# Transposing x by DMA instead of on TensorE for the last five blocks, in a fused window attention and squared-ReLU FFN

## The chip, the cores and the metric

The kernel runs on one core of a Trainium2 chip. The metric is device time in microseconds (us): the median of three runs before the change is 312.11 us (311.29 to 312.19). One more execution was profiled. It took 310.89 us, of which 309.2 us are the span from its first to its last instruction.

## The reference

Causal attention with a window of 64 over 8 batches, 8 heads, 576 positions and a head size of 64 is followed by a feed-forward layer without biases whose activation is the square of a ReLU:

```python
# q, k, v: (8, 8, 576, 64)
scores = (1/8) * q @ k.T                      # masked to 0 <= i - j < 64
attn   = softmax(scores)
x      = (attn @ v).transpose(0, 2, 1, 3).reshape(4608, 512)
out    = maximum(x @ w_in, 0)**2 @ w_out      # w_in 512 x 2048, w_out 2048 x 512
```

The inputs and the output are float32; the kernel works in float16 with float32 sums.

## The kernel before, in words

The 4608 rows are cut into nine blocks of 512 rows, counted from 0 in the code and here. Blocks 0 to 7 are the first 512 positions of each batch; block 8 gathers the last 64 positions of all eight batches. A block's attention consists of four units (g, hp), one for each pair of heads.

A unit passes through these steps. `Sc` forms the scores on TensorE and their exponential on ScalarE. `M` applies the mask on VectorE. `AV` multiplies by v on TensorE. `N` divides by the sum of each row on VectorE and writes the tile `xs`, 128 x 512 in float16, of which there are three buffers. `X` then turns `xs` around: four 128 x 128 transposes on TensorE into PSUM (L323) and one copy of 128 x 512 to the SBUF tile `xT` on ScalarE (helper line L111). `xT[g][:, hp, :]` is the hp-th quarter of the contraction of the first FFN product.

The FFN of a block has 16 groups `F1(g, f)` and 16 groups `F2(g, ts, quarter)`. Each group is four matmuls of 512 columns. An F1 group (L337) needs all four quarters of `xT[g]` in the order of hp; VectorE then takes the ReLU (`hr`, L340) and ScalarE the square (`h2`, L341). Four F2 groups (L372) make one 128 x 512 tile of the output, which ScalarE copies to `osb` (L376, five buffers) and SyncE stores (L362).

The order of all engines is written out by hand. The main loop has passes n = 1 to 8, called stages here. Stage n fills 32 places, counted i = 0 to 31, with the 16 F2 groups of block n and the 16 F1 groups of block n+1, in an order such as `"2222" + "11" + 2 * "212121211" + "21221211"` (1 for F1, 2 for F2). So the first F1 group of a stage stands at place 4. Attention work of block n+2 is put ahead of certain places: `Sc` of units 0 and 1 at place 8, their `AV` and `N` at 14, their `X` at 18 and 20; `Sc` of units 2 and 3 at place 18, their `AV` and `N` at 24, their `X` at 28 and 30. The x of block n+2 is therefore finished in stage n, and stage n+1 reads it from place 4 on.

Three kinds of DMA share the one in-order queue of SyncE (called SP in the profile): loads of the parts of q, k and v (L198, L201, L205), DMA transposes of the cast q and k parts of blocks 3 to 8 (`transpose_part`, L231, 128 x 512 in float16 each), and stores of `osb` (L362). `next_part` issues a load, queues its cast on GpSimd (POOL in the profile), and issues the transpose of the part that was loaded four parts earlier; that transpose waits on SP for the cast. About 14.5 parts are issued in each stage until the 80th part in stage 5. GpSimd does the casts in order, and the shifted copies of v (six a block) between them.

Before the main loop, block 0's F1 groups run in a stage of their own, with the transposes of q and k of block 1's first two units (`T`, L243: eight transposes on TensorE and one copy of 128 x 1024 on ScalarE for unit 0, on VectorE for unit 1) ahead of groups 12 and 14. The change's title counts that block from one, as block 2, and counts block 4 as the fifth.

Of the kernel before, what the change touches and what calls it, by code (L numbers as in the profile page):

```python
# [9 lines left out]
FP16 = mybir.dt.float16  # L10
# [5 lines left out]
def kernel(  # L16
# [6 lines left out]
    moe_w_out: bass.AP,  # L23
    out: bass.AP,
):

    nc = tc.nc  # L30
# [3 lines left out]
    P = 128  # L34
    HP = H // 2
    NBLK = B + 1
    DMC = DM // P
# [12 lines left out]
    xtpool = ctx.enter_context(tc.tile_pool(name="xtpool", bufs=2))  # L50
# [4 lines left out]
    ps_f1 = ctx.enter_context(tc.tile_pool(name="ps_f1", bufs=2, space=bass.MemoryType.PSUM))  # L55
# [53 lines left out]
    def copy(engine, out, in_):  # L109
        if engine is nc.scalar:  # L110
            engine.activation(out=out, in_=in_, func=AF.Copy, scale=1.0)  # L111
        else:
            engine.tensor_copy(out=out, in_=in_)  # L113
# [120 lines left out]
    pm, av, xs, xT = {}, {}, {}, {}  # L234
    at_ps = [ps_at.tile([P, 2, 512], FP32, name=f"at{i}") for i in range(2)]

    def T(g, hp, pool=ps_tr, tag="tr", engine=nc.scalar):

        qkt = apool.tile([P, 2, 512], FP16, name="qk", tag="qk")
        tr = pool.tile([P, 2, 512], FP16, name="tr", tag=tag)  # L240
        for a, what in enumerate("qk"):
            for i in range(4):
                nc.tensor.transpose(out=tr[:, a, i * P:(i + 1) * P],  # L243
                                    in_=p16[what, g, hp][:, i * P:(i + 1) * P], identity=ident[:])
        copy(engine, qkt[:].rearrange("r a (p i) -> r a p i", i=4),
             tr[:].rearrange("r a (i p) -> r a p i", i=4))
        qT[g, hp, "unit"], kT[g, hp, "unit"] = qkt[:, 0, :], qkt[:, 1, :]
# [36 lines left out]
    def M(g, hp):  # L284
        p = pm[g, hp]
        m0 = 1 if g == B else 0
        m = mask[:, m0:m0 + 8, :].rearrange("p j r -> p (j r)")
        nc.vector.tensor_tensor(out=p[:], in0=p[:], in1=m.unsqueeze(1).broadcast_to([P, 2, 512]),  # L288
                                op=ALU.min)
# [27 lines left out]
    def X(g, hp, engine=nc.scalar, pool=ps_tr, tag="tr"):  # L317

        if g not in xT:
            xT[g] = xtpool.tile([P, DMC, 512], FP16, name="xT", tag="xT")  # L320
        tr = pool.tile([P, 2, 512], FP16, name="xtr", tag=tag)
        for jp in range(4):
            nc.tensor.transpose(out=tr[:, 0, jp * P:(jp + 1) * P], in_=xs[g, hp][:, jp, :, :],  # L323
                                identity=ident[:])
        copy(engine, xT[g][:, hp, :], tr[:, 0, :])


    h2 = {}

    def F1(g, f, pool=ps_f1, tag="f1", into=None):  # L330
        if g not in h2:
            h2[g] = h2pool.tile([P, FFC, 512], FP16, name="h2", tag="h2")
        hps, done = open_f1.pop((g, f), (None, 0))
        if hps is None:
            hps = into if into is not None else pool.tile([P, 512], FP32, name="hps", tag=tag)
        for c in range(done, DMC):
            nc.tensor.matmul(hps[:], w_in_sb[:, c, f * P:(f + 1) * P], xT[g][:, c, :],  # L337
                             start=(c == 0), stop=(c == DMC - 1))
        hr = opool.tile([P, 512], FP32, name="hr", tag="hr")
        nc.vector.tensor_scalar(out=hr[:], in0=hps[:], scalar1=0.0, scalar2=None, op0=ALU.max)  # L340
        nc.scalar.activation(out=h2[g][:, f, :], in_=hr[:], func=AF.Square)  # L341
# [26 lines left out]
    def F2(g, ts, quarter, pool, tag):  # L368
        if quarter == 0:
            f2[g, ts] = pool.tile([P, 512], FP32, name="ops", tag=tag)  # L370
        for f in range(4 * quarter, 4 * quarter + 4):
            nc.tensor.matmul(f2[g, ts][:], h2[g][:, f, ts * P:(ts + 1) * P], w_out_sb[:, f, :],  # L372
                             start=(f == 0), stop=(f == FFC - 1))
        if quarter == 3:
            osb = opool.tile([P, DM], FP32, name="osb", tag="osb", bufs=5)
            nc.scalar.activation(out=osb[:], in_=f2[g, ts][:], func=AF.Copy, scale=OUT_SCALE)  # L376
            to_store.append((g, ts, osb))
        if quarter == 1 or g == seq[-1]:
            while to_store:
                store(*to_store.pop(0))  # L380

    def F2_last(g, ts):

        for half, (pool, tag) in enumerate(((ps_f2, "f2"), (ps_f1, "f1"))):
            cols = slice(half * 256, half * 256 + 256)
            t = pool.tile([P, 512], FP32, name="ops", tag=tag)
            for f in range(FFC):
                nc.tensor.matmul(t[:, 0:256], h2[g][:, f, ts * P:(ts + 1) * P], w_out_sb[:, f, cols],  # L388
                                 start=(f == 0), stop=(f == FFC - 1))
            osb = opool.tile([P, DM], FP32, name="osb", tag="osb", bufs=5)  # L390
            nc.scalar.activation(out=osb[:, 0:256], in_=t[:, 0:256], func=AF.Copy, scale=OUT_SCALE)  # L391
            for par, queue in enumerate((nc.sync, nc.scalar)):
                r = (2 * ts + par) * S + 512
                queue.dma_start(out=out[r:r + 64, cols], in_=osb[par * 64:(par + 1) * 64, 0:256])

    seq = list(range(NBLK))
# [3 lines left out]
    with tc.manual_schedule():  # L400
        g0, g1, g2, g3 = seq[:4]
# [17 lines left out]
        dve, pool, act = nc.vector, nc.gpsimd, nc.scalar  # L419
# [59 lines left out]
        three = [in_f1, in_f1, in_f2]  # L479
# [6 lines left out]
            cast_qk_pair(g1, "q", hp, nc.gpsimd)  # L486
            cast_qk_pair(g1, "k", hp, nc.gpsimd)
        for f in range(FFC):
            if f == 12:
                T(g1, 0)  # L490
            if f == 14:
                T(g1, 1, engine=nc.vector)
            F1(g0, f, *three[f % 3])

# [50 lines left out]
        def A(g, hp, i=1):  # L547
            AV(g, hp, i)
            N(g, hp)
# [37 lines left out]
        for n in range(1, NBLK):  # L587
            g = seq[n]
            one = seq[n + 1] if n < NBLK - 1 else None
            if one is not None:  # L590
                first = [lambda f=f: F1(one, f) for f in range(FFC)]
                second = [lambda ts=ts, i=i: F2(g, ts, i, ps_f2, "f2") for ts in range(4) for i in range(4)]
                a, b = iter(first), iter(second)
                order = ("2222" + "11" + 2 * "212121211" + "21221211" if n > 1 else
                         "22222222" + 2 * "11211211212" + "11")
                fill = [next(a if c == "1" else b) for c in order]
            else:
                fill = [lambda ts=ts, i=i: F2(g, ts, i, *((ps_f2, "f2") if ts % 3 == 0 else (ps_f1, "f1")))
                        for ts in range(3) for i in range(4)] + [lambda: F2_last(g, 3)]
            at = {}  # L600

            def put(i, *work):
                at.setdefault(i, []).extend(work)

            if n == 1:
                put(0, lambda: Sc(g2, 3), lambda: A(g2, 2))
                put(2, lambda: M(g2, 3))
                put(3, lambda: X(g2, 2))
                put(4, lambda: A(g2, 3))
                put(6, lambda: X(g2, 3))  # L610
            for work in later:
                put(1, work)
            later = []
            base = 4 * (n + 2)
            for i, x, two in ((12 if n == 1 else 8, (9, 11) if n == 1 else (10, 12), units[base:base + 2]),
                              (21 if n == 1 else 18, (9, None) if n == 1 else (10, 12), units[base + 2:base + 4])):
                for t, u in enumerate(two):
                    if u is not None:
                        put(i, lambda u=u, t=t: Sc(*u, i=t))
                        put(i + 3 + t, lambda u=u: M(*u))  # L620
                        put(i + 6, lambda u=u, t=t: A(*u, i=t))
                        if x[t] is None:
                            later.append(lambda u=u: X(*u))
                        else:
                            put(i + x[t], lambda u=u: X(*u))
            for i, group in enumerate(fill):
                for work in at.pop(i, []):
                    work()
                total = 12 + (32 * (n - 1) + i + 1) * (len(load_list) - 12) // 150
                while done < total and (parts_left or pending):  # L630
                    next_part()
                    done += 1
                group()
            assert not at, at.keys()
# [30 lines left out]
```

## Time and profile before

| | |
|---|---|
| median of three runs | 312.11 us |
| profiled execution: time, span | 310.89 us, 309.2 us |
| TensorE (PE) busy | 299.9 us, 97% of the span |
| VectorE, ScalarE, GpSimd busy | 162.7, 171.6, 117.5 us |
| SP's DMA queue (q1): packets' time, share of 16 engines | 82.8% |
| granted TensorE clock, mean | 1.000 |

The stages 2 to 6 run from 106.9, 138.5, 169.8, 201.1 and 232.5 us of the span, one about 31.35 us after the other, and stage 7 from 263.8 us. TensorE is busy in all of each. The last load of a part is issued at 221.7 us, in stage 5; behind that SP has only stores.

### The profile page before, as it was taken

Reading aid. Unit: us, or ns where it says so; the run is one execution under the profiler, and the core shown is the slowest. Engines: PE = TensorE matmul, PEld = TensorE weight load, DVE = VectorE, ACT = ScalarE, POOL = GpSimd, SP = SyncE. Lnnn points to the kernel's source line nnn. Section 1 sums busy time; section 2 is a strip of 40 time slices with the busy share of each in tenths; the row PEclk is TensorE's granted clock in tenths of the full one; section 3 lists DMA queues with packets and bytes.
Section 4 is the critical chain, followed back from the end, with each engine's and each line's share of the span. In section 5 each row is a group of like instructions: output and inputs, shape, how many; then the busy total and the mean of one; then the engine's idle time right before and its main releaser. Section 6 shows DMA issues by size and latency. Waiting matters only on the chain.

```text
span 309.2 us, 6624 instructions
## 1 busy us (share of the span) xinstructions
PE 299.9 (97%) x2604; PEld 150.8 (49%) x2604; DVE 162.7 (53%) x278; ACT 171.6 (55%) x268; POOL 117.5 (38%) x212
## 2 busy tenths in 40 slices
PE   7899999999999999999999999999999999999995
PEld 5444445454445544544454444544554555444444
DVE  4676628587266727553755365537553655344300
ACT  4757736686367545753575367546744674444411
POOL 4578749963462382254365246322320000000000
PEclk9999999999999999999999999999999999999999
DMA  7999999999999998999998999999921001100023
GB/s 231 241 354 375 384 289 280 310 188 175 235 182 225 178 224 187 204 194 202 197 232 187 211 187 184 205 220 173 217 58 70 34 2 36 68 34 34 36 63 74
DMA packets 141759, 55.49 MB, mean 179 GB/s; under 512 B 125728, under 2 KB 134176, under 8 KB 141728
## 3 DMA queue, kind: packets, MB, share of 16 engines
q1 hardware_dynamic: 141568, 54.94, 82.8%
q8 instruction: 20, 0.33, 0.5%
q10 hardware_dynamic: 160, 0.13, 0.2%
q14 instruction: 11, 0.09, 0.1%
HBM read 38.80 MB, written 9.44 MB: 156 GB/s over the span
## 4 chain that ended last, share of the span: by engine, by line
PE 81%; ACT 0%; DVE 0%; issue 0%
PE hps L337 36%; PE ops L372 35%; PE at L304 3%; PE at L274 3%; PE xtr L323 2%; PE ops L388 1%; PE tr L243 0%; PE hps L353 0%; PE at L337 0%; ACT osb L376 0%; DVE xT L113 0%; ACT osb L391 0%
## 5 line engine op out<-in xcount | busy, mean ns | idle before, releaser
L340 DVE TENSOR_SCALAR hr<-hps 128x512 f32<-128x512 f32 x143 | 97.9, 689 | 107.6 <-PE hps L337 106.4
L341 ACT ACTIVATE h<-hr 128x512 f16<-128x512 f32 x144 | 90.3, 630 | 86.8 <-DVE hr L340 86.6
L337 PE MATMUL hps<-xT,w_in_sb 128*128 128x512 f16 x560 | 137.6, 379 | 0.2
L372 PE MATMUL ops<-w_out_sb,h 128*128 128x512 f16 x560 | 136.1, 379 | 0.3 <-ACT osb L376 0.3
L372 PEld LDWEIGHTS <-h 128*128 128x128 f16 x560 | 53.1, 98 | 61.5 <-issue 0.3
L337 PEld LDWEIGHTS <-w_in_sb 128*128 128x128 f16 x564 | 53.1, 98 | 59.2 <-issue 1.4
L113 POOL CAST v_ev<-st_v 128x512 f16<-128x512 f32 x34 | 23.5, 692 | 43.9 <-DMA st_v<-in_v_dram 43.9
L113 POOL CAST k<-st_k 128x512 f16<-128x512 f32 x36 | 23.1, 641 | 44.7 <-DMA st_k<-in_k_dram 44.4
L281 ACT ACTIVATE pm<-at 128x1024 f16<-128x1024 f32 x35 | 34.1, 1015 | 2.7 <-PE at L274 2.7
L376 ACT ACTIVATE osb<-ops 128x512 f32<-128x512 f32 x35 | 20.5, 587 | 25.2 <-PE ops L372 25.2
L314 DVE TENSOR_TENSOR xs<-at,rden 128x512 f16<-128x512 f32 x36 | 24.9, 691 | 1.2
L288 DVE TENSOR_TENSOR pm<-pm,mask 128x1024 f16<-128x1024 f16 x32 | 24.1, 768 | 2.5 <-ACT pm L281 2.5
L111 ACT ACTIVATE xT<-xtr 128x512 f16<-128x512 f16 x31 | 18.4, 593 | 8.1 <-PE xtr L323 8.1
L113 POOL CAST q<-st_q 128x512 f16<-128x512 f32 x31 | 18.3, 609 | 10.9 <-DMA st_q<-in_q_dram 8.8
L222 POOL CAST v_od<-st_v 64x512 f16<-64x512 f32 x30 | 19.0, 635 | 1.6
L304 PEld LDWEIGHTS <-pm 128*64 128x64 f16 x576 | 11.4, 110 | 8.8 <-issue 4.3
L323 PEld LDWEIGHTS <-xs 128*128 128x128 f16 x144 | 10.7, 98 | 7.5
L304 PE MATMUL at<-v_ev,pm 128*64 128x65 f16 x384 | 14.3, 198 | 0.0
L323 PE MATMUL xtr<-ident,xs 128*128 128x128 f16 x144 | 13.8, 219 | 0.0
L113 POOL CAST v_od<-st_v 64x384 f16<-64x384 f32 x23 | 12.3, 536 | 1.8 <-DMA st_v<-in_v_dram 0.7
L304 PE MATMUL at<-v_od,pm 128*64 128x65 f16 x192 | 10.4, 194 | 0.4 <-DVE v_od L113 0.3
L111 ACT ACTIVATE qk<-tr 128x1024 f16<-128x1024 f16 x7 | 7.1, 1013 | 5.5 <-PE tr L243 3.1
(55 smaller groups left out, 120.4 us busy)
## 6 DMA issues: line engine op xcount, KB each, us to landing
st_k<-in_k_dram SPq DMA_DIRECT2D x40, 256.0 KB, 3.9
st_q<-in_q_dram SPq DMA_DIRECT2D x32, 256.0 KB, 5.1
out_dram<-osb SPq DMA_DIRECT2D x32, 256.0 KB, 2.8
st_v<-in_v_dram SPq DMA_DIRECT2D x28, 256.0 KB, 3.8
st_w<-in_moe_w_out_dram SPq DMA_DIRECT2D x16, 256.0 KB, 5.4
st_v<-in_v_dram SPq DMA_DIRECT2D x24, 128.0 KB, 4.9
w_st<-in_moe_w_in_dram SPq DMA_DIRECT2D x4, 512.0 KB, 6.1
st_w<-in_moe_w_in_dram SPq DMA_DIRECT2D x8, 256.0 KB, 7.6
```

The source lines that it names most:

```text
L111: engine.activation(out=out, in_=in_, func=AF.Copy, scale=1.0)
L113: engine.tensor_copy(out=out, in_=in_)
L281: nc.scalar.activation(out=p[:, hh, :] if apart else p[:], in_=sc[hh] if apart else both[:], func=AF.Exp, scale=1.0 / float(D) ** 0.5)
L288: nc.vector.tensor_tensor(out=p[:], in0=p[:], in1=m.unsqueeze(1).broadcast_to([P, 2, 512]), op=ALU.min)
L304: nc.tensor.matmul(a[jj * 64:(jj + 1) * 64, hh, jp * VW:jp * VW + D + 1], pm[g, hp][:, hh, j * 64:(j + 1) * 64], vsel, start=True, stop=True)
L314: nc.vector.tensor_tensor(out=x[:].rearrange("p j h d -> p h j d"), in0=a[:, :, :, 0:D], in1=rden[:].unsqueeze(3).broadcast_to([P, 2, 4, D ...
L323: nc.tensor.transpose(out=tr[:, 0, jp * P:(jp + 1) * P], in_=xs[g, hp][:, jp, :, :], identity=ident[:])
L337: nc.tensor.matmul(hps[:], w_in_sb[:, c, f * P:(f + 1) * P], xT[g][:, c, :], start=(c == 0), stop=(c == DMC - 1))
L340: nc.vector.tensor_scalar(out=hr[:], in0=hps[:], scalar1=0.0, scalar2=None, op0=ALU.max)
L341: nc.scalar.activation(out=h2[g][:, f, :], in_=hr[:], func=AF.Square)
L372: nc.tensor.matmul(f2[g, ts][:], h2[g][:, f, ts * P:(ts + 1) * P], w_out_sb[:, f, :], start=(f == 0), stop=(f == FFC - 1))
L376: nc.scalar.activation(out=osb[:], in_=f2[g, ts][:], func=AF.Copy, scale=OUT_SCALE)
```

## The change

- In stages 2 to 6 (blocks 4 to 8, twenty units) `X` is replaced by `X_dma`: one DMA transpose on SP's queue, from `xs` straight into `xT`. It stands at places 16 and 17 for units 0 and 1 and at places 26 and 27 for units 2 and 3, ahead of the parts and stores of its place. The four TensorE transposes and the ScalarE copy of these units are gone.
- In block 0's F1 stage, `T` of block 1's units 0 and 1 is issued from inside `F1`, after the matmuls of groups 12 and 14 and before their ReLU and square, where it stood ahead of those matmuls.

```diff
+    def X_dma(g, hp):
+        if g not in xT:
+            xT[g] = xtpool.tile([P, DMC, 512], FP16, name="xT", tag="xT")
+        nc.sync.dma_start_transpose(
+            out=xT[g][:, hp, :].rearrange("p (j r) -> p j r", j=4),
+            in_=xs[g, hp][:].rearrange("p j h d -> p (j h d)"))
...
-    def F1(g, f, pool=ps_f1, tag="f1", into=None):
+    def F1(g, f, pool=ps_f1, tag="f1", into=None, then=None):
...
         for c in range(done, DMC):
             nc.tensor.matmul(hps[:], w_in_sb[:, c, f * P:(f + 1) * P], xT[g][:, c, :],
                              start=(c == 0), stop=(c == DMC - 1))
+        if then is not None:
+            then()
         hr = opool.tile([P, 512], FP32, name="hr", tag="hr")
...
         for f in range(FFC):
-            if f == 12:
-                T(g1, 0)
-            if f == 14:
-                T(g1, 1, engine=nc.vector)
-            F1(g0, f, *three[f % 3])
+            F1(g0, f, *three[f % 3], then={12: lambda: T(g1, 0), 14: lambda: T(g1, 1)}.get(f))
...
-                        if x[t] is None:
+                        if u[0] >= seq[4]:
+                            put(i + 8 + t, lambda u=u: X_dma(*u))
+                        elif x[t] is None:
                             later.append(lambda u=u: X(*u))
```

Before, `T` of unit 1 was copied by VectorE; in the new call it takes the default engine, ScalarE.

## The prediction

> **What bounds the kernel now.** I read the page first, for the busy shares and the chain that ended last, then the main stages window by window, then TensorE's timeline around the removed work, and last SP's own timeline and waits, because the change puts its work there.
>
> ```profile
> PE 299.9 (97%) x2604; PEld 150.8 (49%) x2604; DVE 162.7 (53%) x278; ACT 171.6 (55%) x268; POOL 117.5 (38%) x212
> DMA  7999999999999998999998999999921001100023
> PE hps L337 36%; PE ops L372 35%; PE at L304 3%; PE at L274 3%; PE xtr L323 2%; PE ops L388 1%; PE tr L243 0%; PE hps L353 0%; PE at L337 0%; ACT osb L376 0%; DVE xT L113 0%; ACT osb L391 0%
> L111 ACT ACTIVATE xT<-xtr 128x512 f16<-128x512 f16 x31 | 18.4, 593 | 8.1 <-PE xtr L323 8.1
> ...
> qT<-q SPq DMA_TRANSPOSE x24, 3.5
> ```
>
> TensorE is the bound: 97% busy, and the chain that ended last is matmuls throughout, the x transposes (L323) 2% of it. What leaves TensorE is time gained, as long as nothing makes it wait. But the row of DMA digits is full up to slice 29, and only then falls. The windows of stages 4, 5 and 6 say the same:
>
> ```profile
> 169.96:201.30 31.34, 31.34 (x273) 15.37 (x272) 16.49 (x28) 17.67 (x29) 13.26 (x23) 1.00 1.10 197
> 201.30:232.65 31.35, 31.35 (x273) 15.41 (x272) 17.14 (x28) 17.64 (x29) 8.39 (x14) 1.00 0.94 162
> 232.65:264.00 31.35, 31.35 (x273) 15.41 (x272) 16.50 (x28) 17.67 (x29) 0.00 (x0) 1.00 0.10 35
> ```
>
> The last columns are granted clock, DMA share and GB/s: the DMA engines have packets in flight all the time up to stage 5, almost none in stage 6. TensorE's timeline shows a removed step, and the one stall that the second part touches:
>
> ```profile
> 126.69 0.39 PE L323 MATMUL xtr<-ident,xs 128*128 128x128 f16 x4
> 126.91 1.03 PE L337 MATMUL hps<-xT,w_in_sb 128*128 128x512 f16 x4
> ```
>
> ```profile
> 28.97 0.40 PE L243 MATMUL tr<-ident,q 128*128 128x128 f16 x4
> 29.71 0.40 PE L243 MATMUL tr<-ident,k 128*128 128x128 f16 x4 [0.35 <-POOL k L113]
> ```
>
> Four transposes take 0.22 us from start to the next start. SP's timeline in stages 2 and 4 shows no slack of that kind:
>
> ```profile
> 136.18 1.68 SPq L198 DMA_DIRECT2D st_k<-in_k_dram  x1
> 139.93 1.19 SPq L231 DMA_TRANSPOSE qT<-q  x1
> ...
> 189.21 2.88 SPq L231 DMA_TRANSPOSE qT<-q  x1
> 192.14 0.57 SPq L205 DMA_DIRECT2D st_k<-in_k_dram  x1
> 192.81 1.21 SPq L231 DMA_TRANSPOSE qT<-q  x1
> 194.06 0.58 SPq L205 DMA_DIRECT2D st_k<-in_k_dram  x1
> 194.75 1.21 SPq L231 DMA_TRANSPOSE qT<-q  x1
> 196.05 0.52 SPq L362 DMA_DIRECT2D out_dram<-osb  x1
> 196.63 0.42 SPq L205 DMA_DIRECT2D st_k<-in_k_dram  x1
> ```
>
> SP issues without a pause. A load and a transpose take 1.92 us (192.14 to 194.06), the load with its gap 0.62, so a transpose costs SP 1.30 us. Three things stretch this: a wait for a cast on GpSimd (137.9 to 139.9), and issues held to several times their length (1.68, 2.88) while earlier transfers are still in flight. And SP is late: the store at 196.05 stands behind place 26 of stage 4, which TensorE began at 195.51, though its tile had been ready at 192.58. A queue with slack would have sent it then, as it does from stage 6 on.
>
> **The second part of the change.** Moving `T` behind group 12's matmuls takes away the 0.35 us that TensorE waits for GpSimd's cast of k; with the gaps about 0.4 us. For unit 1 the copy moves from VectorE (1.21 us at 32.55) to ScalarE (about 1.0, 30.22); its transposes start 0.2 us later than now, the copy ends at about 33.6, and the scores of unit 1 would be due at about 33.5. So they wait 0.1 to 0.3 us, and the squares of groups 14 and 15 come 1 us later, which is hidden: the first F2 groups read groups 0 to 3. Ends: 0.6 gained, or 0.2 lost if the scores wait longest. I take 0.4 gained.
>
> **The removed work.** 20 units x 0.22 us = 4.4 us off TensorE, all on the chain. Twenty ScalarE copies of 0.593 us go too; ScalarE is 55% busy and nothing waits for it there, so they count nothing. Together 4.8 us.
>
> **The added work.** Twenty transposes of 128 x 512, the shape of the q and k parts, so 1.30 us of SP each. The four of stage 6 are free: SP then waits for most of the stage. The other sixteen lie in a full queue. None waits long for `N`: SP is behind TensorE at places 16 and 17 and, once delayed, at 26 and 27 too. What is behind them is every later load, transpose and store. Loads come 14 places or more before their unit needs them, stores have five buffers; the first to be late is the x itself. Unit 3 of a block is issued at place 27 and read by the fourth matmul of place 4 of the next stage.
>
> The tightest place is the start of stage 5. In the row of 196.05 SP has reached place 26 of stage 4; the next issue is at 196.63. By then it will have issued 4 + 4 + 4 new transposes, 12 x 1.30 = 15.6 us: unit 3's issue ends at 212.2, and the shortest landing in this stretch is 1.2 us after the end of an issue, so 213.4. TensorE wants it at 204.59 (start of place 4) + 3 x 0.216 = 205.2, less 12 x 0.22 and 0.4 gained by then: 202.2. That is 11.2 us late if SP's stretched spots stay as they are.
>
> They can shrink. Between 122 (the first new issue) and 196 SP waits for casts 2.0 us (137.9) and 1.65 (162.5), and is held 1.7 (132.5), 1.35 (to 137.9), 0.55 (148), 2.4 (158 to 162), 1.3 (177) and 1.65 (189.2) beyond the plain length: 12.6 us in all. An added issue that falls into such a spot costs nothing. So the wait of TensorE lies between 0 (11.2 absorbed) and 11.2 us (none), and the change breaks even where 6.4 of the 12.6 us, half, are absorbed. I take three tenths, 3.8 us. The holds come from the DMA engines being full, and a transpose brings 0.55 us of its own there (in a string of landings a transpose comes 0.5 to 0.6 us behind the load before it), so at most 0.75 of 1.30 can vanish in a hold, and only about half of the new issues stand in or just ahead of one. The waits for casts move along, because the loads that feed those casts are delayed in the same queue. That gives 11.2 - 3.8 = 7.4 us.
>
> The same sum for stage 4 (store at 165.48, next issue 166.06, 8 new transposes, wanted at 171.7) gives 177.7, 6.0 late, less 2.9 = 3.1 us; this wait is part of the 7.4, since TensorE's waiting does not slow SP. For stage 3 it gives 0, for stage 6 at most 0.2 more.
>
> **Sum.** -4.8 + 7.4 = +2.6 us. The profiled execution would go from 310.89 to 313.5. The median is 1.2 us above that execution, so 312.1 becomes 314.7 us.
>
> On SP's price the Trainium skill, page "DMA: Bandwidth & Descriptors", section "Issuing engines are not separate DMA queues", says that the time a sequencer takes to start a DMA is usually small beside the DMA. The rows differ (1.21 us of issue, 0.55 us between landings). By that rule the twelve transposes would cost 12 x 0.55 = 6.6 us in place of 15.6, 2.2 late unabsorbed, and the time would be that of the first rival.
>
> **Rivals.**
> *SP takes it up (faster).* If over half of the 12.6 us is absorbed, TensorE waits under 4.8 us; with all of it, not at all, and the time is 312.1 - 4.8 = 307.3. For it: the new issues at places 26 and 27 of stage 2 stand right in the string of held loads and ahead of the wait of 139.93. Against it: SP was late at every store of stages 2 to 5 but two.
> *The waits also cost the clock.* No wait of TensorE after its first 1.5 us is longer than 0.5 us now. The forecast's two (3.1 and then 4.3) would be the first long ones. At its start TensorE issued 24 matmuls of 128 x 128 in 2.74 us, 0.114 each against 0.055 in the x transposes, and was slow for about 4 us. If it starts so again twice, 2 us are lost each time: 314.7 + 4 = 318.7. The Trainium skill, page "TensorE: Matmul & The Clock Gate", part 1, states that an idle window of about 3.4 us halves the clock; no run here shows it in mid-kernel.
> *The three `xs` buffers bind.* Unit 3's `N` reuses unit 0's buffer, so VectorE would wait for unit 0's transpose. In stage 4 by the same sums it lands at about 196.0, with `N` due at 195.5; F1's two PSUM banks cover that. It adds 1 to 2 us where SP absorbs nothing, 312.1 - 4.8 + 11.2 + 1.5 = 320.
>
> **How the numbers follow.** Forecast case (TensorE waits 6 to 11.2 us): 0.50, time 314.7, own range 313.2 to 318.5. SP takes it up: 0.29, 307.3 to 311.1. Near balance, within 0.3% (about 0.9 us, what a measurement of this kernel can tell from no change): 0.08. Clock or buffers on top: 0.13, 318.7 to 320. So faster 0.29, same 0.08, slower 0.63. The range 307.5 to 319 leaves out the last tail and a sliver at the low end.
>
> **What would show it.** Right: L323 falls from 144 to 64 matmuls; waits of TensorE at L337 for the DMA that writes `xT`, at the starts of stages 4 and 5, some 3 and 4 us; the last load issued well after 221.7 us; stage 6 about 0.9 us shorter. Wrong: no such waits and stages of 30.5 us (first rival); matmuls of an F1 group at 0.43 us behind a wait (second); VectorE's `xs` waiting for a DMA (third). If a new transpose costs SP much more or less than 1.30 us, the whole sum moves by twelve times that.

## The result, and the profile after

| | before | changed |
|---|---|---|
| median (lowest to highest), us | 312.15 (311.23 to 312.52), 6 runs | 316.01 (313.5 to 317.55), 6 runs |
| profiled execution: time, span, us | 310.89, 309.2 | 316.02, 314.1 |
| granted TensorE clock, mean, profiled execution | 1.000 | 0.989 |

The ratio of the times is 1.0126, with an interval of 1.008 to 1.0173: the changed kernel is 1.3% slower. The two profiled executions differ by 5.1 us, the medians by 3.9, because the profiled execution of before lay 1.2 us under its median and that of after lies on it.

The page of the changed kernel: busy time by engine, the slices of TensorE, its granted clock and the DMA engines, the last chain by line, and two groups.

```profile
PE 299.2 (95%) x2524; PEld 146.7 (47%) x2524; DVE 161.9 (52%) x277; ACT 162.9 (52%) x249; POOL 117.0 (37%) x212
PE   6999998999999999999999699969999999999995
PEclk9999999999999999999999799989999999999999
DMA  6999999999999999999999999999999022101123
PE hps L346 32%; PE ops L383 29%; DMA xT<-xs 3%; DMA st_q<-in_q_dram 3%; PE at L275 3%; PE at L305 3%; PE ops L399 1%; DVE hr L351 1%; PE xtr L324 1%; SPq L332 1%; DVE pm L289 1%; SPq L373 1%; SPq L232 1%; ACT h L352 1%; PE tr L244 0%
L346 PE MATMUL hps<-xT,w_in_sb 128*128 128x512 f16 x560 | 140.2, 383 | 5.9 <-DMA xT<-xs 5.5
L112 ACT ACTIVATE xT<-xtr 128x512 f16<-128x512 f16 x11 | 6.5, 594 | 5.6 <-PE xtr L324 5.6
```

TensorE issues 80 instructions fewer and is busy for about the same time, 299.2 against 299.9 us, although the removed transposes were worth 4.4. So some of the rest ran slower. The row of TensorE has two dips (slices 22 and 26, counted from 0; the starts of stages 4 and 5), the row of its granted clock has two in the same slices, the DMA row stays full for two slices longer, and ScalarE's copies into `xT` (L112) fall from 31 to 11. The last chain is no longer matmuls throughout: the new transpose (`DMA xT<-xs`) and SP's issues are in it.

Stages 4, 5 and 6 of the changed kernel, window by window (length, the busy time of each engine with its instructions, and at the end granted clock, DMA share, GB/s):

```profile
168.40:203.42 35.02, 32.38 (x257) 14.87 (x256) 17.53 (x28) 15.66 (x25) 13.84 (x24) 0.95 1.05 191
203.42:238.55 35.13, 32.33 (x258) 14.74 (x256) 16.63 (x28) 15.65 (x25) 8.96 (x16) 0.95 1.18 193
238.55:269.00 30.45, 30.45 (x257) 14.41 (x256) 16.50 (x28) 15.66 (x25) 1.23 (x2) 1.00 0.28 73
```

Each lasted 31.35 us before. Stage 6 is 0.90 us shorter: four units without their TensorE transposes, 4 x 0.22. Stages 4 and 5 are 3.7 and 3.8 us longer. TensorE's timeline at their starts (start, duration, operation; in brackets the idle time ahead of it and what ended that):

```profile
171.69 0.81 PE L346 MATMUL hps<-xT,w_in_sb 128*128 128x512 f16 x3
175.14 1.96 PE L346 MATMUL hps<-xT,w_in_sb 128*128 128x512 f16 x5 [2.64 <-DMA xT<-xs]
176.89 1.91 PE L383 MATMUL ops<-w_out_sb,h 128*128 128x512 f16 x4
...
206.71 0.59 PE L346 MATMUL hps<-xT,w_in_sb 128*128 128x512 f16 x2
208.07 0.38 PE L346 MATMUL hps<-xT,w_in_sb 128*128 128x512 f16 x1 [0.76 <-DMA xT<-xs]
210.26 2.29 PE L346 MATMUL hps<-xT,w_in_sb 128*128 128x512 f16 x5 [1.82 <-DMA xT<-xs]
```

In stage 4 three matmuls of the first F1 group run, and the fourth waits for unit 3's quarter of `xT`. In stage 5 the third waits too. The matmuls behind the waits are slow: four of L383 take 1.91 us, which take 1.03 elsewhere. The granted clock in windows around them says why:

```profile
175.50:178.90 3.40, 3.40 (x10) 1.18 (x8) 1.38 (x2) 1.26 (x2) 0.70 (x2) 0.50 0.88 174
179.00:182.40 3.40, 3.40 (x46) 1.69 (x45) 0.79 (x2) 1.78 (x3) 1.21 (x4) 1.00 1.11 264
209.60:213.00 3.40, 2.74 (x7) 1.01 (x7) 1.03 (x2) 0.63 (x1) 0.61 (x1) 0.51 0.78 172
213.10:216.50 3.40, 3.40 (x46) 1.71 (x45) 0.94 (x2) 1.70 (x3) 0.86 (x2) 1.00 1.27 224
```

Half clock for about 3.4 us, twice, and full clock behind it. On SP, around place 26 of stage 4 (its store is the one at 206.88, which before stood at 196.05):

```profile
203.94 1.20 SPq L232 DMA_TRANSPOSE qT<-q  x1
205.24 1.21 SPq L332 DMA_TRANSPOSE xT<-xs  x1
206.88 0.36 SPq L373 DMA_DIRECT2D out_dram<-osb  x1
207.35 1.29 SPq L332 DMA_TRANSPOSE xT<-xs  x1
208.68 0.57 SPq L206 DMA_DIRECT2D st_k<-in_k_dram  x1
```

The two new transposes (L332) cost SP 1.21 and 1.29 us, as much as one of q (1.20). The second is unit 3's of block 6. It lands at 210.22, and TensorE had begun place 4 at 206.71; it waits for unit 2's first, the transpose issued at 205.24, and then for this one.

**Where the time went.** I compared the start of every FFN group in the two profiled executions. TensorE is 0.15 us ahead at the start of stage 1, 0.22 by its end, and gains another 0.22 at each of the twenty places where a unit's transposes are gone (4.4 in all). It loses 0.45 us at place 4 of stage 3, 2.8 in the wait of stage 4, 1.7 at half clock behind it, 2.9 in the waits of stage 5, 1.4 at half clock, 0.4 at places 29 and 30 of stage 5, and 0.1 elsewhere: 9.7 lost, 4.7 gained, 5.0 in the sum. The spans differ by 4.9.

### The profile page after: what moved, and what is told of

It reads as the page before. It is cut to its first block, busy times and chain, and to the rows that moved or that the text cites. A ratio compares the mean times of both kernels' runs of the same rounds, so it can differ in the third digit from the quotient of the medians.

```text
span 314.1 us, 6501 instructions
## 1 busy us (share of the span) xinstructions
PE 299.2 (95%) x2524; PEld 146.7 (47%) x2524; DVE 161.9 (52%) x277; ACT 162.9 (52%) x249; POOL 117.0 (37%) x212
## 3 DMA queue, kind: packets, MB, share of 16 engines
q1 hardware_dynamic: 152448, 57.56, 86.9%
## 4 chain that ended last, share of the span: by engine, by line
PE 69%; DMA 6%; SPq 3%; DVE 2%; issue 1%; ACT 1%; POOL 0%; DVEq 0%; POOLq 0%
PE hps L346 32%; PE ops L383 29%; DMA xT<-xs 3%; DMA st_q<-in_q_dram 3%; PE at L275 3%; PE at L305 3%; PE ops L399 1%; DVE hr L351 1%; PE xtr L324 1%; SPq L332 1%; DVE pm L289 1%; SPq L373 1%; SPq L232 1%; ACT h L352 1%; PE tr L244 0%
## 5 line engine op out<-in xcount | busy, mean ns | idle before, releaser
L346 PE MATMUL hps<-xT,w_in_sb 128*128 128x512 f16 x560 | 140.2, 383 | 5.9 <-DMA xT<-xs 5.5
L383 PE MATMUL ops<-w_out_sb,h 128*128 128x512 f16 x560 | 137.3, 382 | 0.3 <-ACT osb L387 0.3
L346 PEld LDWEIGHTS <-w_in_sb 128*128 128x128 f16 x564 | 54.1, 98 | 70.4 <-issue 10.6
L383 PEld LDWEIGHTS <-h 128*128 128x128 f16 x560 | 53.4, 98 | 62.8 <-issue 2.4
L114 POOL CAST v_ev<-st_v 128x512 f16<-128x512 f32 x34 | 21.7, 638 | 49.6 <-DMA st_v<-in_v_dram 49.6
L282 ACT ACTIVATE pm<-at 128x1024 f16<-128x1024 f32 x35 | 34.1, 1013 | 2.8 <-PE at L275 2.8
L387 ACT ACTIVATE osb<-ops 128x512 f32<-128x512 f32 x35 | 20.6, 588 | 25.0 <-PE ops L383 25.0
L114 POOL CAST q<-st_q 128x512 f16<-128x512 f32 x31 | 19.1, 626 | 18.8 <-DMA st_q<-in_q_dram 15.7
L112 ACT ACTIVATE qk<-tr 128x1024 f16<-128x1024 f16 x8 | 8.1, 1016 | 5.4 <-PE tr L244 3.3
L112 ACT ACTIVATE xT<-xtr 128x512 f16<-128x512 f16 x11 | 6.5, 594 | 5.6 <-PE xtr L324 5.6
L312 DVE RECIPROCAL rden<-at 128x8 f32<-128x8 f32 x36 | 7.2, 200 | 3.7 <-PE at L305 3.5
L114 POOL CAST w_out_sb<-st_w 128x512 f16<-128x512 f32 x12 | 7.7, 642 | 3.1 <-DMA st_w<-in_moe_w_out_dram 2.7
```

Source lines behind the costliest of these rows:

```text
L282: nc.scalar.activation(out=p[:, hh, :] if apart else p[:], in_=sc[hh] if apart else both[:], func=AF.Exp, scale=1.0 / float(D) ** 0.5)
```

## The experiments

The theory after the result: SP's queue was full, each new transpose costs it a fixed time of issue, so the x of blocks 5 and 6 lands too late, and TensorE waits and then runs at half clock. Its rivals: that the transposes are late because of their bytes on the DMA engines and not because of their issue, that the clock would have fallen anyway, and that the moved `T` is what costs time. The kernel before ran beside every kernel, with medians of 312.15 (experiments 1 to 4), 311.98 (5 to 8) and 312.43 us (9 and 10).

**1. The moved `T` alone.** All x stays on TensorE.

```diff
-                        if u[0] >= seq[4]:
+                        if False:
```

> The changed kernel with x of all units transposed on TensorE as before, so that only the moved transposes of block 1 are left of the change. Theory: TensorE loses its 0.35 us wait at L243 and nothing else changes; in the trace of the changed kernel stage 1 begins 0.15 us earlier than before, so 311.7 to 312.1 us, no measurable difference. Rival: the two ScalarE copies ahead of the squares hold back later work, and this part of the change is to blame for some of the loss: 312.6 us or more.

Measured: 312.94 us (312.14 to 314.27), ratio 1.003 (1.0014 to 1.0046). It is not faster, against the forecast, and it lies outside the 311.7 to 312.1 us expected, in the range given for the rival (312.6 or more). TensorE's timeline of this kernel around the moved transposes:

```profile
30.33 0.39 PE L244 MATMUL tr<-ident,q 128*128 128x128 f16 x4
30.90 0.40 PE L244 MATMUL tr<-ident,k 128*128 128x128 f16 x4 [0.18 <-POOL k L114]
31.13 1.89 PE L346 MATMUL hps<-xT,w_in_sb 128*128 128x512 f16 x8
```

`T` stands 1.4 us later than before (28.97) and TensorE still reaches k before its cast is done, because in this execution GpSimd did that cast 1.2 us later (30.23 in place of 29.04). Stage 1 starts 0.5 us later than before, and the remaining 1.4 us of this execution's loss lie behind the last matmuls, where the last but one store took 2.58 us to issue on ScalarE's queue (0.56 before), which has nothing to do with `T`. In ten profiled executions of this study (all but experiment 9's) stage 1 starts anywhere from 0.15 us earlier to 1.5 us later than before, under both orders. A gain of 0.4 us can't be seen in that, and the rival isn't shown by it either.

**2. Each new transpose in two halves.** The same bytes, twice the issues.

```diff
-        nc.sync.dma_start_transpose(
-            out=xT[g][:, hp, :].rearrange("p (j r) -> p j r", j=4),
-            in_=xs[g, hp][:].rearrange("p j h d -> p (j h d)"))
+        for a in (0, 2):
+            nc.sync.dma_start_transpose(
+                out=xT[g][:, hp, a * P:(a + 2) * P].rearrange("p (j r) -> p j r", j=2),
+                in_=xs[g, hp][:, a:a + 2].rearrange("p j h d -> p (j h d)"))
```

> The changed kernel with each new DMA transpose issued as two of 128 x 256: the same bytes and packets, twice the issues on SP. Theory (SP's issue time is what runs out): each half still costs SP about 1.2 us, so unit 3 of block 6 lands about 12 x 1.2 = 14 us later than in the changed kernel, less what falls into holds; 324 to 332 us, with the waits at the starts of stages 4 to 6 several us longer. Rival (the DMA engines' time runs out): the bytes are the same, 315 to 318 us.

Measured: 336.6 us (335.24 to 337.6), ratio 1.0782 (1.0752 to 1.0812). SP's timeline of this kernel at place 26 of stage 4, then the wait of TensorE for `xT` (total, times, longest):

```profile
214.90 1.20 SPq L232 DMA_TRANSPOSE qT<-q  x1
216.15 0.58 SPq L206 DMA_DIRECT2D st_k<-in_k_dram  x1
216.82 1.21 SPq L232 DMA_TRANSPOSE qT<-q  x1
218.13 2.48 SPq L333 DMA_TRANSPOSE xT<-xs  x2
220.71 0.53 SPq L374 DMA_DIRECT2D out_dram<-osb  x1
```

```profile
PE hps L347 <- DMA xT<-xs: 19.4, 8, 4.7
```

Two halves take 2.48 us, 1.24 each, where a whole one takes 1.22. Sixteen extra issues in stages 2 to 5 are 20 us of SP, and TensorE's waits for `xT` grow from 5.5 to 19.4; more of it runs at half clock too (mean 0.959). The time is above the 324 to 332 us expected, which had counted twelve of the issues and no further loss of clock. No byte was added, and the packets of SP's queue took no longer on the DMA engines: 78.1% of 335.6 us is 262 us, against 86.9% of 314.1, or 273 us, in the changed kernel. So the issue on SP is what is scarce. The Trainium skill, page "DMA: Bandwidth & Descriptors", section "Issuing engines are not separate DMA queues", calls the time to start a DMA usually small beside the DMA itself; for this transpose the measurement decides otherwise.

**3. The stores of blocks 1 to 5 on ScalarE's queue**, to free SP of 20 stores.

```diff
-            nc.sync.dma_start(out=out[g * S + ts * P:g * S + (ts + 1) * P, :], in_=osb[:])
+            (nc.scalar if 1 <= g <= 5 else nc.sync).dma_start(
+                out=out[g * S + ts * P:g * S + (ts + 1) * P, :], in_=osb[:])
```

> The changed kernel with the stores of blocks 1 to 5 issued from ScalarE's queue in place of SP's. They use the same 16 DMA engines. Theory (SP's issue time): ten stores of 0.58 us stand ahead of the late transpose at the start of stage 5, so it comes 5.8 us earlier; of the 8.0 us by which it landed too late about 2 are left, too short to lose the clock: 308.5 to 311 us, clock 1.00. Rival (DMA engines): the same packets pass through the same engines, 315 to 317.5 us, waits as in the changed kernel.

Measured: 317.27 us (316.0 to 317.62), ratio 1.0158 (1.0137 to 1.0179). The expectation failed. ScalarE's timeline of this kernel in stage 1:

```profile
78.89 0.60 ACT L388 ACTIVATE osb<-ops 128x512 f32<-128x512 f32 x1 [0.27 <-PE ops L384]
86.69 0.39 ACTq L373 DMA_DIRECT2D out_dram<-osb  x1
87.12 0.60 ACT L112 ACTIVATE xT<-xtr 128x512 f16<-128x512 f16 x1 [7.64 <-DMA st_q<-in_q_dram]
```

The first store on ScalarE's queue was held until 86.6 us, when a load that SP had issued landed, and everything behind it on ScalarE stood for 7.64 us. In the trace that load and the store report their landing on the same semaphore, and the wait ahead of the store is for that semaphore: the program as built asked for it, and it is no property of ScalarE's queue. TensorE lost 3.9 us waiting for the `xT` copy and about 1.7 more at half clock. So from stage 2 on the kernel runs some 6 us later than SP's loads were planned for, and the disappearance of the wait in stage 4 can't be credited to the freed queue. As a test of SP this run is inconclusive.

**4. TensorE kept busy where it waits.** 13 and 20 matmuls without use ahead of place 4 of stages 4 and 5; they are extra work, their result goes nowhere.

```diff
+    def fill_pe(n):
+        t = ps_tr.tile([P, 512], FP32, name="fill", tag="tr")
+        for _ in range(n):
+            nc.tensor.matmul(t[:], ident[:], w_in_sb[:, 0, 0:512], start=True, stop=True)
...
+                if i == 4 and n in (4, 5):
+                    fill_pe({4: 13, 5: 20}[n])
```

> The changed kernel with idle TensorE time filled: 13 matmuls of 512 columns into a spare PSUM bank ahead of place 4 of stage 4 and 20 ahead of place 4 of stage 5, results unused. Theory (the slow matmuls behind each wait are the clock, lost by standing idle): the clock stays at 1.00 and the matmuls behind the waits keep 0.216 us. The first loss (1.7 us) is hidden in the lateness of the next transpose anyway, so about 1.4 us are won: 314.6 us against 316.0. Rival (matmuls behind a wait are slow for another reason, such as the transfers): they stay slow, and the fill adds up to 1 us: 316 to 317 us.

Measured: 314.46 us (313.89 to 315.55), ratio 1.0069 (1.005 to 1.0088), with a granted clock of 1.000 in every run. TensorE's timeline of this kernel at the start of stage 4:

```profile
172.91 2.97 PE L357 MATMUL fill<-w_in_sb,ident 128*128 128x512 f16 x13
175.71 2.02 PE L346 MATMUL hps<-xT,w_in_sb 128*128 128x512 f16 x8
177.57 1.03 PE L388 MATMUL ops<-w_out_sb,h 128*128 128x512 f16 x4
```

Behind the filler the four L388 matmuls take 1.03 us in place of 1.91. So the half clock follows from the waits and is not there anyway. By the medians, work without use makes the kernel 1.5 us faster than the changed one (316.01), though the intervals of the two ratios overlap a little. That is about the price of one of the two slow spells, not of both (3.1); the section on the prediction says why. In this execution, the slowest of the four at 315.55, the second filler ran too long: unit 3's x had landed at 210.24, and the fourth matmul of place 4 came at 211.26, so about 1.0 us of the gain was given away.

**5. The x transposes alone**, `T` put back where it was.

```diff
-            F1(g0, f, *three[f % 3], then={12: lambda: T(g1, 0), 14: lambda: T(g1, 1)}.get(f))
+            if f == 12:
+                T(g1, 0)
+            if f == 14:
+                T(g1, 1, engine=nc.vector)
+            F1(g0, f, *three[f % 3])
```

> The changed kernel with block 1's transposes put back ahead of the matmuls of groups 12 and 14 and copied as before, so that only x by DMA is left. If the moved transposes cost the 0.8 us that the run of them alone showed, this takes 315.2 us; if that run's loss was chance (half of it lay in its last stores), 316 us. Theory on the rest unchanged: waits of TensorE for the DMA into xT at the starts of stages 4 and 5, each followed by 3.4 us at half clock.

Measured: 316.56 us (314.84 to 316.78), ratio 1.0126 (1.0092 to 1.0161), the ratio of the whole change. The loss is that of the x transposes. The slow spells didn't come as expected: in the profiled execution the wait of stage 4 is 0.83 us and brings none, and behind waits of 2.94 and 1.72 us in stage 5 the clock is at half for 6.8 us, from 207.2 to 214.0.

**6. One transpose for two units.** `xs` becomes two double tiles of 128 x 1024 (`osb` goes from five buffers to four to make room), and at places 17 and 27 one DMA transposes both units.

```diff
+        if hp % 2:
+            nc.sync.dma_start_transpose(
+                out=xT[g][:, hp - 1:hp + 1, :].rearrange("p u (j r) -> p (u j) r", j=4),
+                in_=xs2[g, hp - 1][:].rearrange("p u j h d -> p (u j h d)"))
```

> The changed kernel with one DMA transpose of 128 x 1024 for two units, at places 17 and 27 (two xs buffers for two units each, and four osb buffers to make room): the same bytes, half the issues. Theory (a transpose costs SP 1.2 us whatever its size, as the halves of the split run did): six issues fewer stand ahead of the start of stage 5, 7.8 us, and the lateness of 8.0 us is gone, the lost clock with it: 307.8 to 310 us. If the cost grows with the size, or if the DMA engines are what is short: 315 to 317 us.

Measured: 308.35 us (307.41 to 309.86), ratio 0.9884 (0.985 to 0.9918). SP and TensorE of this kernel around the start of stage 5:

```profile
199.41 1.21 SPq L232 DMA_TRANSPOSE qT<-q  x1
200.72 0.54 SPq L375 DMA_DIRECT2D out_dram<-osb  x1
201.35 1.29 SPq L334 DMA_TRANSPOSE xT<-xs  x1
202.69 0.57 SPq L206 DMA_DIRECT2D st_k<-in_k_dram  x1
```

```profile
202.89 0.59 PE L348 MATMUL hps<-xT,w_in_sb 128*128 128x512 f16 x2
204.78 1.45 PE L348 MATMUL hps<-xT,w_in_sb 128*128 128x512 f16 x6 [1.30 <-DMA xT<-xs]
```

Twice the size costs SP 1.29 us, hardly more than one unit's. With ten issues in place of twenty the same bytes and the same work off TensorE make the kernel faster than before; one wait of 1.3 us is left, without a fall of the clock. With experiment 2 this shows it from both sides: doubled issues cost 20.6 us, halved ones gain 7.7, with the packets' time on the DMA engines about the same in all three (262, 273 and, 88.1% of 307.0, 270 us).

**7. The new transposes for block 8 only** (stage 6, where SP has little to do), `T` as before.

```diff
-                        if u[0] >= seq[4]:
+                        if u[0] >= seq[8]:
```

> The kernel before with x by DMA for block 8 alone (stage 6, where SP only waits for stores). Theory: the step itself wins what TensorE sheds, 4 x 0.22 = 0.9 us: 311.3 us, no waits. Rival (the DMA path is slow in itself, landing late even on an idle queue): a wait at the start of stage 7 and 312 us or more.

Measured: 310.73 us (309.93 to 311.44), ratio 0.9968 (0.9942 to 0.9994). TensorE waits for no `xT`, and gains 0.89 us in stage 6. A transpose is free where the queue is idle, as the prediction had it for stage 6.

**8. The parts spread more thinly**, over 164 places in place of 150, so that fewer stand ahead of the x.

```diff
-                total = 12 + (32 * (n - 1) + i + 1) * (len(load_list) - 12) // 150
+                total = 12 + (32 * (n - 1) + i + 1) * (len(load_list) - 12) // 164
```

> The changed kernel with the parts of q, k and v spread to the start of stage 6 (164 places in place of 150): nothing of x changes, but by place 26 of stage 4 SP has some 4.5 parts less behind it, about 9 us of issues, and by place 26 of stage 3 3.5 parts, 6.7 us. Theory: no waits at the starts of stages 4 and 5; at the start of stage 6, which the late parts now crowd, up to 4 us: 309 to 312 us. Rival (the new transposes themselves are slow, whatever stands ahead of them): 315 to 317 us, waits in the same places.

Measured: 314.04 us (311.6 to 316.0), ratio 1.0058 (1.0027 to 1.0089): by the median 2.0 us better than the changed kernel, with intervals that overlap a little, but above what was expected. The wait of stage 4 is gone in the profiled execution; one of 1.4 us is left in stage 5, and a new one stands at the start of stage 6, since the parts now run on into it. That one is of use for the clock:

```profile
234.25 0.81 PE L346 MATMUL hps<-xT,w_in_sb 128*128 128x512 f16 x3
237.93 1.24 PE L346 MATMUL hps<-xT,w_in_sb 128*128 128x512 f16 x5 [2.87 <-DMA xT<-xs]
239.01 1.03 PE L383 MATMUL ops<-w_out_sb,h 128*128 128x512 f16 x4
```

It is longer than the 2.64 us of the changed kernel, and the matmuls behind it run at full clock. But this execution was the fastest of ten (311.6 us, mean clock 0.997), and one more, at 1.000, took 311.87; the other eight, with mean clocks of 0.988 to 0.995, took 312.93 to 316.0 us. So the waits that are left seem to cost a spell or two in most executions, which would put the median above the 309 to 312 us expected; those executions have no trace.

**9 and 10. The pair of experiment 6 and the parts over 160 places**, with `T` moved (9) and with `T` as before (10). The edits are those of experiments 6 and 8, with 160 for 164, and for the second that of 5.

> One transpose for two units as before in this study, and the parts of q, k and v spread over 160 places in place of 150. Theory: by place 26 of stage 4 SP has 3.6 parts less behind it, so the 1.5 us that TensorE still waited at the start of stage 5 go; at the start of stage 6 eight issues fewer stand ahead than in the run with spread parts alone, 10 us against the 3.0 us of wait there: no wait. All of the 4.4 us is won: 307 to 308 us, clock 1.00. Rival: spreading the parts makes block 8's q and k late for stage 6: a wait at its scores, 309 us or more.

> The same with block 1's transposes put back as they were before the change. With no wait for x left, the difference between this run and the one beside it is the second part of the change alone. My prediction said 0.4 us won by moving them; the run of that part alone said 0.8 us lost. I expect neither: within 0.5 us of the run beside it, 307 to 308 us.

Measured: 307.32 us (306.34 to 307.58), ratio 0.9838 (0.9814 to 0.9861), and 307.89 us (307.54 to 308.47), ratio 0.9869 (0.9843 to 0.9894). In the profiled execution of the second TensorE never waits for `xT`, and it gains 0.22 us at each of the twenty places, 4.5 in all. It begins its stages with two groups in one run (L348 is `F1`'s matmul there):

```profile
200.79 2.54 PE L385 MATMUL ops<-w_out_sb,h 128*128 128x512 f16 x11
203.17 1.89 PE L348 MATMUL hps<-xT,w_in_sb 128*128 128x512 f16 x8
```

This is all that the removed work can give, and the version of experiment 9 has the lowest median of the study, 1.6% faster than before. The two differ by 0.57 us with overlapping intervals; within 0.5 was expected. A fifth execution of experiment 9, the profiled one, took 775.78 us, with TensorE busy for 769.0 us and its FFN matmuls slow throughout (831 ns in the mean, 379 before). Nothing on record says why; it is left out, and experiment 9 has no trace that could be read.

## Why the prediction was right or wrong

The direction, the places and the cause were right: slower, by waits for unit 3's x at the starts of stages 4 and 5, since SP had no time for the new issues. The forecast said 314.7, the median is 316.01. The step that failed is the sum -4.8 + 7.4, which had no term for the clock; that stood among the rivals. Part of the agreement is luck: the forecast carried over the 1.2 us by which the median before lay above its profiled execution, and for the changed kernel the two are the same. Between the profiled executions +2.6 was forecast and +5.1 came, a miss of 2.5 us where the medians show 1.3.

- *Removed work, 4.4 us.* Right: 0.22 us at each of twenty places.
- *SP's price, 1.30 us.* Right: 1.22 us at the median and its gap. That the price is one of the issue and not of the bytes was argued from one row; experiments 2 and 6 show it.
- *Lateness at stage 5, 11.2 us unabsorbed.* Unit 3's issue ended at 208.64 in place of 212.2, so 3.6 us were absorbed (3.8 forecast). It landed 1.6 us later (1.2 forecast), at 210.22: 8.0 us behind 202.2, where the forecast had 7.4.
- *Waits of 7.4 us, 3.1 and 4.3.* Measured 6.15 (0.45, 2.8 and 2.9 us). With the first slow spell (1.7) TensorE had lost 7.85 us by then, which is the lateness. So the first slow spell cost nothing by itself: a slower TensorE came to the next late x later, and waited less for it. Experiment 4 shows this: with no spell in stage 4, unit 3's x in stage 5 landed at 210.24, in the changed kernel at 210.22. Only the last spell, 1.4 us, is on top of the lateness. This is why taking away both in experiment 4 could gain about 1.4 us and not 3.1. Its profiled execution ends only 0.5 us earlier than that of the changed kernel, about the 1.4 less the 1.0 us that its filler ran over; the 1.5 us between the medians fit no better than that.
- *"The waits also cost the clock"* came true, at 1.7 and 1.4 us in place of 2 each. The forecast priced it as an addition of 4; by the point above it adds 1.4. Of the six runs two had a mean clock of 0.995, as one spell would give (3.41 x 0.5 / 314 = 0.0054); they took 313.5 and 315.1 us, the four others, at 0.987 to 0.989, took 316.0 to 317.55.
- *"The three `xs` buffers bind"*, said to be covered by F1's two PSUM banks. Mostly: VectorE waited 2.82 us for unit 0's transpose in stage 5 (its timeline below), and TensorE lost 0.4 us by it, waiting for `hr` at 236.64.

```profile
232.28 0.20 DVE L312 RECIPROCAL rden<-at 128x8 f32<-128x8 f32 x1
235.29 0.69 DVE L315 TENSOR_TENSOR xs<-at,rden 128x512 f16<-128x512 f32 x1 [2.82 <-DMA xT<-xs]
```

- *Second part, 0.4 us gained.* Not shown. The profiled execution of the changed kernel had 0.15 to 0.2, experiment 1 lost 0.8 us (0.4 to 1.4 by its interval), experiment 9 stands 0.57 us ahead of 10, and experiment 5 shows no difference. Its sign stays open; all of it lies within 1.4 us. What experiment 1's profiled execution lost beside `T`, the late store at its end, was not followed up.

In the terms of the forecast: +2.6, then 0.6 for the lateness, 1.4 for the last slow spell, 0.4 for VectorE and 0.2 for the smaller gain at the start give +5.2; TensorE's matmuls in stage 7 stand 5.0 us later.

## What to carry to other kernels

Before moving work from a full engine to a DMA, look at the queue that issues it: here the price was 1.2 to 1.3 us of SP for each transpose, from 128 x 256 to 128 x 1024, so fewer and larger ones turned a loss of 1.3% into a gain of 1.2% with the same work removed. Judge the queue by its late stores and not by a busy share (the packets of SP's queue took 88.1% of the DMA engines' time in experiment 6 and 86.9% in the slower changed kernel), and put new issues where it idles. Where a chain of data is late by a fixed amount, losses ahead of it (waits, slow clock) are paid out of that lateness, and only what comes behind the last late item adds to it.

## What the runs showed of the hardware that was not expected

- A DMA transpose held SP for 1.24 us at 128 x 256, 1.22 at 128 x 512 and 1.28 at 128 x 1024 (medians).
- In the changed kernel the granted clock fell to half for 3.41 us at a time (175.5 to 178.9 and 209.6 to 213.0), in experiment 5 once for 6.8 us, and not for every long wait: TensorE was idle for 2.64 us ahead of the first and for 0.76 and 1.82 around the second, yet 2.87 us in experiment 8 brought none. The two spells begin 34.1 us apart, ten times 3.41. The Trainium skill, page "TensorE: Matmul & The Clock Gate", part 1, states a free-running window of 3413 ns, and this fits it: what would count is how much idle time falls into one window of a fixed grid. No experiment was made for this, but the traces bear it out. Below are the 3.41 us ahead of each spell of the changed kernel, and the two windows over which the wait of experiment 8 falls. The edges of these last two are counted in steps of 3.413 us back from 308.02, where its clock fell after the last matmul. In each line the second number is TensorE's busy time.

```profile
172.10:175.51 3.41, 0.77 (x4) 0.29 (x3) 0.00 (x0) 0.44 (x1) 0.61 (x1) 1.00 0.89 215
206.24:209.65 3.41, 1.44 (x6) 0.49 (x5) 0.00 (x0) 0.60 (x1) 0.61 (x1) 1.00 0.91 169
232.93:236.34 3.41, 2.13 (x10) 0.88 (x9) 0.00 (x0) 0.60 (x1) 0.83 (x2) 1.00 0.84 190
236.34:239.75 3.41, 1.82 (x9) 0.87 (x9) 1.16 (x2) 0.61 (x1) 0.49 (x2) 1.00 0.85 197
```

TensorE was idle in 2.64 and 1.97 us of the first two, and half clock followed; in experiment 8 the grid splits the wait into 1.28 and 1.59 us, and none followed. In all traces but experiment 9's, cut in this way, half clock followed every window at full clock with more than 1.9 us idle, and none with less than 1.6. So a window need not be idle throughout, and by this the same wait can cost a spell in one execution and none in the next.

- A store moved to ScalarE's queue stopped ScalarE for 7.64 us (experiment 3), because it shared a semaphore with a load on SP's queue that had not landed. That came from how the program hands out its semaphores and not from the chip, but it doesn't show in the source line that moves the store.
